# Expert token places cut from 256 to 240 in a fused linear-attention and mixture-of-experts kernel

## The chip, the cores and the metric

The kernel runs on one core of a Trainium2 chip. The metric is the device time of one execution in microseconds (us), and the time given for a kernel is the median of several runs. All profile times below are us from the start of the profiled span unless ns is written. PE is the matmul engine TensorE and PEld its weight load, DVE is VectorE, ACT is ScalarE, POOL is GpSimd, and SP is the engine that issues most transfers.

## The reference

A recurrence over 768 steps runs for 4 batches and 8 heads of width 48, and its output is read as 3072 tokens of 384 numbers. These tokens go through a mixture of 8 experts. A token is worked on only if its skip score is above zero. It then belongs to one expert, the one of the largest gate logit.

```
state = w_t * state + k_t v_t^T          # per batch and head, 768 steps
y_t   = r_t (state_before + (u * k_t) v_t^T)

do_compute = x @ w_skip > 0              # x: 3072 x 384
e_idx  = argmax(x @ w_gate)              # 8 experts
gate_w = softmax(x @ w_gate)[e_idx]
h      = max(x[mask_e] @ w1[e], 0)       # 384 -> 1024
y      = gate_w * (h @ w2[e])            # 1024 -> 384
out[do_compute] = x + y
```

Worked out from these lines and the inputs that the reference draws, 1514 of the 3072 tokens are worked on, and the eight experts get 194, 234, 156, 201, 198, 219, 156 and 156 of them.

## The kernel before

The first part of the kernel goes through 24 chunks of 128 tokens and computes the recurrence, the outputs and the gate logits. While it does so, a router gives every token that is worked on a place in its expert: place 0, 1, 2 and so on, in the order of the tokens. There are two tiles of 128 places for each expert, 256 in all (`CAP`). The list of tokens by place is `idr` for reading and `ids` for writing.

The second part is the experts, and the change touches only this part. `expert(e)` runs for e from 0 to 7. For each expert the tokens are gathered row by row from `out` by an indirect transfer (`gather`), one transfer for each tile `xg` of 128 places. `tokens(e)` turns the two tiles around on PE (`psX`, three transposes a tile) and splits the result into a high part `xTh` and a low part `xTl`, both of the type float32r (f32r). Weights are split in the same way by `split_slice`, 512 columns at a time, into `w1h`, `w1l`, `w2h` and `w2l`.

The first layer has 8 blocks `psH` of 128 hidden units. Each block is 9 matmuls (three 128-deep slices by the three products high*high, high*low, low*high), with a 128x128 block of weights as the stationary operand and 256 token columns as the moving one. ACT takes a finished block out of PSUM as `hh`, and DVE makes the low part `hl` from the same block. Four PSUM banks take turns for `psH`, so a block needs the bank that the block four before it left. The second layer is `psO`: for each of the two token tiles 24 matmuls with 128 token columns of `hh` or `hl` as the stationary operand and 384 columns of `w2` as the moving one. DVE then forms `fin` (gate times the sum, plus the token), and `scatter` on POOL writes the rows back to `out`.

Expert 0 is different. Its first 128 places are done ahead of time (`early_expert`), and its second tile uses plain float32 matmuls (`hidden`, line 133 in the profile).

The order of PE, ACT, DVE and POOL in this part is the order of the code. The weights of the expert after next are loaded by SP when the splits have left the raw tile.

Two tests at the end decide whether a slow general path runs instead. One of them asks whether any token's place is `CAP` or higher (`row_tests`). With the inputs drawn it is not taken.

Of the kernel before, what the change touches and what calls it, by code (L numbers as in the profile page):

```python
# [8 lines left out]
F32 = mybir.dt.float32  # L9
BF16 = mybir.dt.bfloat16  # L10
F32R = mybir.dt.float32r
# [10 lines left out]
P = 128  # L22
NT = B * S
# [4 lines left out]
NP = H // 2  # L28
KC = DM // P
FC = DF // P  # L30
CAP = 256
CW = P + 2
Q_MIN = 2.0 ** -60
TOL = 2e-5
# [1 line left out]
NHB = 11  # L36
# [20 lines left out]
def rwkv_moe_kernel(ctx, tc, wrk, wrk0, vN, uP, wgs, wgp, w12, cst, out):  # L57
    nc = tc.nc
# [28 lines left out]
    def split(dst_h, dst_l, src, eng=None):  # L87
        nc.scalar.copy(dst_h, src)  # L88
        (eng or nc.vector).tensor_tensor(dst_l, src, dst_h.bitcast(F32), op=ALU.subtract)  # L89

    def split_slice(e, i, eng=None):
        q, cs = i // 6, slice((i % 6) * 512, (i % 6 + 1) * 512)
        for k in (2 * q, 2 * q + 1):
            if (e, k) not in wsp:
                wtile(e, k)
        split(wsp[e, 2 * q][:, cs], wsp[e, 2 * q + 1][:, cs], raws[e, q][:, cs], eng)
# [20 lines left out]
    def drain(g):  # L117
        for _ in g:
            pass
# [3 lines left out]
    xg = {s: keep.tile([P, DM], F32, name=f"xg{s}") for s in range(4)}  # L123
# [7 lines left out]
    def hidden(ps, xT, fc, kc):  # L131
        o = kc * DF + fc * P
        return nc.tensor.matmul(ps, raws[0, 0][:, o:o + P], xT[:, kc], start=(kc == 0),  # L133
                                stop=(kc == KC - 1))
# [5 lines left out]
    with tc.tile_pool(name="att", bufs=2) as att, \  # L140
# [51 lines left out]
        ident = c_sb[:, C_ID:C_ID + P]  # L192
# [243 lines left out]

        idr = keep.tile([P, 2, E], U32, name="idr")

        def gather(s, pool):
            if pool:  # L440
                xg[s] = pool.tile([P, DM], F32, tag=f"xg{s}", name=f"xg{s}", bufs=1)
            return nc.gpsimd.indirect_dma_start(
                out=xg[s], out_offset=None, in_=out,
                in_offset=bass.IndirectOffsetOnAxis(ap=idr[:, s % 2, s // 2:s // 2 + 1], axis=0),
                bounds_check=NT - 1, oob_is_err=False)

        def router(i0, m):
# [319 lines left out]
        ids = keep.tile([P, 2, E], U32, name="ids")  # L767
        gates = keep.tile([P, 2, E], F32, name="gates")
        with tc.manual_schedule(engines={nc.tensor.engine, nc.scalar.engine, nc.vector.engine}):
# [9 lines left out]
            for k in range(done[0], 6 * FC - 4):  # L779
# [4 lines left out]
                                    axis=AX, op=ALU.add)  # L784
# [5 lines left out]
    with tc.tile_pool(name="wset1", bufs=1) as ws1, tc.tile_pool(name="moe", bufs=2) as moe, \  # L790
            tc.tile_pool(name="ps2", bufs=1, space=PSUM) as ps2:
        wset1[0] = ws1
        def pair(e, instr=None):
            for s in (2 * e, 2 * e + 1):
                ga = gather(s, moe)
                if instr is not None:
                    tc.add_manual_dep(ga.ins, instr.ins.name,
                                      mybir.DependencyInfo(mybir.DependencyClass.Sync,
                                                           mybir.DependencyReason.DATA),
                                      reason="pace")  # L800
# [8 lines left out]
        def tokens(e):  # L809
            xTh = moe.tile([P, KC, CAP], F32R, tag="xTh", name=f"xTh{e}")  # L810
            xTl = moe.tile([P, KC, CAP], F32R, tag="xTl", name=f"xTl{e}")
            for j in range(2):
                ps = ps1.tile([P, KC, P], F32, tag="psT", name=f"psX2{e}_{j}", bufs=2)
                for kc in range(KC):
                    nc.tensor.transpose(ps[:, kc], xg[2 * e + j][:, kc * P:(kc + 1) * P], ident)  # L815
                split(xTh[:, :, j * P:(j + 1) * P], xTl[:, :, j * P:(j + 1) * P], ps)
            xTs[e] = xTh, xTl

        def scatter(s, o):
            sc = nc.gpsimd.indirect_dma_start(  # L820
                out=out, out_offset=bass.IndirectOffsetOnAxis(ap=ids[:, s % 2, s // 2:s // 2 + 1],
                                                               axis=0),
                in_=o, in_offset=None, bounds_check=NT - 1, oob_is_err=False)
            tc.declare_no_dep(sc.ins, group="rows", reason="tokens are scattered to rows of their own")
            tc.add_to_no_dep_group("rows", sc.ins)

# [4 lines left out]
        def row_tests():  # L831
# [10 lines left out]
            nc.vector.tensor_reduce(vt[:, 2:3], rall[:, :, 0], axis=AX, op=ALU.max)  # L842
            nc.vector.tensor_scalar(vt[:, 2:3], vt[:, 2:3], float(CAP), None, op0=ALU.is_ge)
            nc.vector.scalar_tensor_tensor(vt[:, 3:4], vt[:, 1:2], B * NC - 0.5, vt[:, 2:3],
# [8 lines left out]
        def expert(e):  # L853
            todo = []
            if e + 1 < E:
                todo = list(range(0 if e > 0 else 6, 12))

            def more(k):
                for _ in range(k):
                    if todo:  # L860
                        split_slice(e + 1, todo.pop(0))


            h = {}
            nh = FC if e > 0 else FC // 2
            for q in range(nh):
                ps = (ps1 if q % 4 < 2 else ps2).tile(
                    [P, CAP], F32, tag=("psA0", "psA1", "psY", "psB")[q % 4], name=f"psH{e}_{q}")
                hh = moe.tile([P, CAP], F32R, tag="hh", name=f"hh{e}_{q}", bufs=NHB)
                hl = moe.tile([P, CAP], F32R, tag="hl", name=f"hl{e}_{q}", bufs=NHB)  # L870
                if e == 0:
                    for i in range(2):
                        ts = slice(i * P, (i + 1) * P)
                        for kc in range(KC):
                            hidden(ps[:, ts], xT0[1], 2 * q + i, kc)
                        h[1, 2 * q + i] = hh[:, ts], hl[:, ts]
                else:
                    w1h, w1l = wsp[e, 0], wsp[e, 1]
                    xTh, xTl = xTs[e]
                    for kc in range(KC):  # L880
                        o = kc * DF + q * P
                        nc.tensor.matmul(ps, w1h[:, o:o + P], xTh[:, kc], start=(kc == 0), stop=False)  # L882
                        nc.tensor.matmul(ps, w1h[:, o:o + P], xTl[:, kc], start=False, stop=False)  # L883
                        nc.tensor.matmul(ps, w1l[:, o:o + P], xTh[:, kc], start=False,  # L884
                                         stop=(kc == KC - 1))
                    for j in range(2):
                        ts = slice(j * P, (j + 1) * P)
                        h[j, q] = hh[:, ts], hl[:, ts]
                act = nc.scalar.activation(hh, ps, AF.Relu)  # L889
                if later_pairs and (e, q) != (0, 0):  # L890
                    pair(later_pairs.pop(0), act)
                    while first and not later_pairs:
                        scatter(*first.pop(0))
                nc.vector.scalar_tensor_tensor(hl, ps, 0.0, hh.bitcast(F32),  # L894
                                               op0=ALU.max, op1=ALU.subtract)
                more(1)
            if e + 1 < E:
                tokens(e + 1)
            if e == 0:
                first.append((0, fin0))  # L900
            w2h, w2l = wsp[e, 2], wsp[e, 3]
            for j in range(1 if e == 0 else 0, 2):
                pso = ps1.tile([P, DM], F32, tag=("psu", "pss")[j], name=f"psO{e}_{j}")
                for fc in range(FC):
                    o = slice(fc * DM, (fc + 1) * DM)
                    nc.tensor.matmul(pso, h[j, fc][0], w2h[:, o], start=(fc == 0), stop=False)  # L906
                    nc.tensor.matmul(pso, h[j, fc][0], w2l[:, o], start=False, stop=False)  # L907
                    nc.tensor.matmul(pso, h[j, fc][1], w2h[:, o], start=False,  # L908
                                     stop=(fc == FC - 1))
                more(2)  # L910
                if j == 0 and e in (1, 2):
                    (row_tests, verdict)[e - 1]()
                s = 2 * e + j
                o = moe.tile([P, DM], F32, tag="fin", name=f"fin{e}_{j}", bufs=3)
                nc.vector.scalar_tensor_tensor(o, pso, gates[:, j, e:e + 1], xg[s],  # L915
                                               op0=ALU.mult, op1=ALU.add)
                if later_pairs:
                    first.append((s, o))
                else:
                    scatter(s, o)  # L920
                if s == 2 * E - 3:
                    nc.gpsimd.drain()
                    verdicts.append(nc.values_load(flag_i[0:1, 0:1], min_val=0, max_val=2))
            more(12)
            if e + 2 < E:
                drain(load_weights(e + 2, 0))
                drain(load_weights(e + 2, 1))
# [170 lines left out]
```

## Time and profile before

| what | value |
|---|---|
| median of 3 runs | 286.65 us (286.0 to 287.15) |
| the profiled execution | 286.06 us |
| its span, first to last instruction | 284.2 us |
| PE busy | 271.2 us, 95% of the span |
| granted TensorE clock over the span | 0.999 of full speed |
| DVE, ACT, POOL busy | 217.0, 159.4, 145.9 us |
| memory traffic | 64.41 MB, mean 227 GB/s |

1.86 us of the profiled execution lie outside its span. The experts 1 to 7 take the stretch from 156.0 to 279.3 us. A matmul's record begins before the array is free for it, so the records of neighbours overlap; how long one matmul takes in a row of them is read from the distance of their starts, and not from the duration in the record. A plain float32 matmul leaves two records, each with a weight load of its own (48 such matmuls at line 133 stand as x96).

### The profile page before, as it was taken

The numbers are of one execution on the slowest core, as the hardware profiler recorded it, in microseconds if no ns is written. First come the engines' busy times: TensorE is split into PE (matmuls) and PEld (weight loads), VectorE is DVE, ScalarE is ACT, GpSimd is POOL, SyncE is SP. The second block draws the span as 40 slices with busy tenths as digits, with TensorE's granted clock in tenths as the row PEclk, the third lists the DMA queues.
The fourth block names the chain that finished last, engine by engine and source line by source line (L and its number), as shares of the span: only waits on it lengthen the run. The fifth ranks groups of instructions, "written<-read, shape, count | busy, mean of one in ns | idle before, by whom it ended". The sixth has DMA issues, their size and how long they took to land.

```text
span 284.2 us, 8967 instructions
## 1 busy us (share of the span) xinstructions
PE 271.2 (95%) x3601; PEld 248.9 (88%) x3602; DVE 217.0 (76%) x414; ACT 159.4 (56%) x464; POOL 145.9 (51%) x140
## 2 busy tenths in 40 slices
PE   6998999999999999999999999999999999999993
PEld 2687878788887888887999999999999999999992
DVE  7997999999989999972747697948859588595320
ACT  5175555787658957768416573827638276381310
POOL 4986775699978998974656625011030110201111
PEclk9999999999999999999999999999999999999999
DMA  7999999998999869992078997565672656700001
GB/s 217 239 311 333 277 345 339 363 332 246 297 278 302 252 218 348 308 310 65 28 256 294 345 314 267 212 213 200 221 258 68 231 200 221 268 5 28 10 5 41
DMA packets 26131, 64.41 MB, mean 227 GB/s; under 512 B 4342, under 2 KB 15386, under 8 KB 26080
## 3 DMA queue, kind: packets, MB, share of 16 engines
q1 hardware_dynamic: 23712, 58.14, 62.3%
q0 software_dynamic: 2048, 5.48, 5.9%
q8 instruction: 30, 0.49, 0.7%
q10 hardware_dynamic: 320, 0.13, 0.2%
q14 instruction: 21, 0.17, 0.2%
HBM read 56.69 MB, written 7.86 MB: 227 GB/s over the span
## 4 chain that ended last, share of the span: by engine, by line
PE 57%; POOL 8%; issue 6%; DVE 4%; ACT 3%; DMA 1%; POOLq 0%; DVEq 0%; ACTq 0%
PE psH L884 7%; PE psH L883 7%; PE psH L882 7%; PE psO L906 6%; PE psO L908 6%; PE psO L907 6%; PE psH L133 4%; PE psY L409 3%; POOL rp L336 2%; PE psA L358 2%; POOL kq L326 2%; PE psY L413 2%; PE psX L815 2%; PE psO L658 2%; PE psX L425 1%
## 5 line engine op out<-in xcount | busy, mean ns | idle before, releaser
L820 POOL DMA_INDIRECT out<-fin,ids x16 | 16.8, 1047 | 99.1 <-DVE fin L915 92.7
L889 ACT ACTIVATE hh<-psH 128x256 fp32r<-128x256 f32 x60 | 23.1, 385 | 56.6 <-PE psH L884 53.4
L884 PE MATMUL psH<-xTh,w1l 128*128 128x256 f32 x168 | 47.5, 283 | 0.0
L883 PE MATMUL psH<-xTl,w1h 128*128 128x256 f32 x168 | 47.5, 283 | 0.0
L882 PE MATMUL psH<-xTh,w1h 128*128 128x256 f32 x168 | 47.5, 283 | 0.0
L906 PE MATMUL psO<-w2h,hh 128*128 128x384 f32 x120 | 40.9, 341 | 0.0
L908 PE MATMUL psO<-w2h,hl 128*128 128x384 f32 x120 | 40.2, 335 | 0.0
L907 PE MATMUL psO<-w2l,hh 128*128 128x384 f32 x120 | 40.1, 335 | 0.0
L894 DVE SCALAR_TENSOR_TENSOR hl<-psH,hh 128x256 fp32r<-128x256 f32 x60 | 25.1, 418 | 13.3 <-ACT hh L889 12.0
L326 POOL TENSOR_TENSOR kq<-wrk,q 128x512 f32<-128x512 f32 x24 | 28.2, 1177 | 11.7 <-DVE q L309 3.5
L364 DVE TENSOR_TENSOR asb<-psA,c_sb 128x512 f32<-128x512 f32 x48 | 30.4, 676 | 3.5 <-PE psA L358 3.4
L331 DVE TENSOR_TENSOR_SCAN rh<-wrk,rowsk,pss 128x520 f32<-128x520 f32 x24 | 31.1, 1296 | 2.0
L318 POOL TENSOR_TENSOR rk<-wrk 128x512 f32<-128x512 f32 x24 | 31.0, 1292 | 2.4 <-DMA wrk<-wrk 2.4
L884 PEld LDWEIGHTS psH<-xTh,w1l 128*128 128x128 f32 x168 | 32.2, 192 | 0.0
L883 PEld LDWEIGHTS psH<-xTl,w1h 128*128 128x128 f32 x168 | 32.2, 192 | 0.0
L882 PEld LDWEIGHTS psH<-xTh,w1h 128*128 128x128 f32 x168 | 32.2, 191 | 0.0
L309 DVE TENSOR_TENSOR_SCAN q<-wrk,pss 128x520 f32<-128x520 f32 x24 | 29.5, 1230 | 3.0 <-DMA wrk<-wrk 0.9
L336 POOL TENSOR_TENSOR rp<-wrk,rh 128x512 f32<-128x512 f32 x23 | 27.2, 1181 | 5.4 <-DVE rh L331 5.0
L89 DVE TENSOR_TENSOR w2l<-r,w2h 128x512 fp32r<-128x512 f32 x42 | 27.7, 685 | 2.0 <-ACT w2h L88 1.4
L409 PE MATMUL psY<-asb,v 128*48 128x128 f32 x384 | 26.5, 276 | 2.6 <-DVE psY L381 2.3
L915 DVE SCALAR_TENSOR_TENSOR fin<-psO,gates,xg 128x384 f32<-128x384 f32 x15 | 9.3, 618 | 25.2 <-PE psO L908 24.6
L358 PE MATMUL psA<-rp,kq 64*64 64x128 f32 (+1 forms) x768 | 26.0, 251 | 1.8 <-issue 1.1
(154 smaller groups left out, 608.4 us busy)
## 6 DMA issues: line engine op xcount, KB each, us to landing
r<-w SPq DMA_DIRECT2D x48, 512.0 KB
wrk<-wrk SPq DMA_DIRECT2D x21, 772.5 KB
v<-vN SPq DMA_DIRECT2D x24, 192.0 KB
vt<-wrk SPq DMA_DIRECT2D x48, 96.0 KB
out<-x SPq DMA_DIRECT2D x24, 192.0 KB
wrk<-wrk SPq DMA_DIRECT2D x1, 579.4 KB
wrk<-wrk SPq DMA_DIRECT2D x1, 512.0 KB
wrk<-wrk SPq DMA_DIRECT2D x1, 384.0 KB
```

Source lines behind the costliest of these rows:

```text
L318: nc.gpsimd.tensor_tensor(work[i]["rk"].rearrange("p a j -> p (a j)"), t[:, R_OFF:K_OFF], t[:, K_OFF:V_OFF], op=ALU.mult)
L326: nc.gpsimd.tensor_tensor(kq, wk["k"], wk["q"][:, :, 1:1 + P], op=ALU.mult)
L331: nc.vector.tensor_tensor_scan(rh.rearrange("p a j -> p (a j)"), wk["w"][:, 0:NP * CW], reads_at[:, :NP * CW], rowsk, op0=ALU.mult, op1=AL ...
L336: eng.tensor_tensor(rp, wk["r"], rh[:, :, :P], op=ALU.mult)
L358: nc.tensor.matmul(psa[g][j:j + HP, a, j:], wk["kq"][rows, a, j:j + HP], wk["rp"][rows, a, j:], start=True, stop=True)
L409: nc.tensor.matmul(y_at(a, g), v[:, 2 * a + g], wk["asb"][g][:, a], start=False, stop=True, skip_group_check=True)
L882: nc.tensor.matmul(ps, w1h[:, o:o + P], xTh[:, kc], start=(kc == 0), stop=False)
L883: nc.tensor.matmul(ps, w1h[:, o:o + P], xTl[:, kc], start=False, stop=False)
L884: nc.tensor.matmul(ps, w1l[:, o:o + P], xTh[:, kc], start=False, stop=(kc == KC - 1))
L906: nc.tensor.matmul(pso, h[j, fc][0], w2h[:, o], start=(fc == 0), stop=False)
L907: nc.tensor.matmul(pso, h[j, fc][0], w2l[:, o], start=False, stop=False)
L908: nc.tensor.matmul(pso, h[j, fc][1], w2h[:, o], start=False, stop=(fc == FC - 1))
```

## The change

The constant `CAP` becomes 240. The first tile of an expert keeps 128 places and the second has 112. For the experts 1 to 7 everything that ran over 256 token columns runs over 240, and everything that ran over the second tile runs over 112 rows: the gather, the transposes, the two splits, the first layer's matmuls, `hh` and `hl`, the stationary operand of the second tile's `psO`, `fin` and the scatter. Expert 0 keeps 256 columns. The list of places still has 256 entries, of which the last 16 are not gathered. The test for the general path now asks for a place of 240 or higher.

```diff
-CAP = 256
+CAP = 240
...
+        def width(j):
+            return min(P, CAP - j * P)
+
         def gather(s, pool):
...
+            w = width(s % 2) if s > 1 else P
             return nc.gpsimd.indirect_dma_start(
-                out=xg[s], out_offset=None, in_=out,
-                in_offset=bass.IndirectOffsetOnAxis(ap=idr[:, s % 2, s // 2:s // 2 + 1], axis=0),
+                out=xg[s][:w], out_offset=None, in_=out,
+                in_offset=bass.IndirectOffsetOnAxis(ap=idr[:w, s % 2, s // 2:s // 2 + 1], axis=0),
...
-                    nc.tensor.transpose(ps[:, kc], xg[2 * e + j][:, kc * P:(kc + 1) * P], ident)
-                split(xTh[:, :, j * P:(j + 1) * P], xTl[:, :, j * P:(j + 1) * P], ps)
+                    nc.tensor.transpose(ps[:, kc, :w], xg[2 * e + j][:w, kc * P:(kc + 1) * P],
+                                        ident[:w, :w])
+                split(xTh[:, :, ts], xTl[:, :, ts], ps[:, :, :w])
...
         def scatter(s, o):
+            w = width(s % 2)
...
-                in_=o, in_offset=None, bounds_check=NT - 1, oob_is_err=False)
+                in_=o[:w], in_offset=None, bounds_check=NT - 1, oob_is_err=False)
...
+            n_ = CAP if e > 0 else 2 * P
...
-                    [P, CAP], F32, tag=("psA0", "psA1", "psY", "psB")[q % 4], name=f"psH{e}_{q}")
-                hh = moe.tile([P, CAP], F32R, tag="hh", name=f"hh{e}_{q}", bufs=NHB)
-                hl = moe.tile([P, CAP], F32R, tag="hl", name=f"hl{e}_{q}", bufs=NHB)
+                    [P, n_], F32, tag=("psA0", "psA1", "psY", "psB")[q % 4], name=f"psH{e}_{q}")
+                hh = moe.tile([P, 2 * P], F32R, tag="hh", name=f"hh{e}_{q}", bufs=NHB)[:, :n_]
+                hl = moe.tile([P, 2 * P], F32R, tag="hl", name=f"hl{e}_{q}", bufs=NHB)[:, :n_]
...
+                w = width(j) if e > 0 else P
+                po = pso[:w]
...
-                    nc.tensor.matmul(pso, h[j, fc][0], w2h[:, o], start=(fc == 0), stop=False)
+                    nc.tensor.matmul(po, h[j, fc][0], w2h[:, o], start=(fc == 0), stop=False)
...
-                nc.vector.scalar_tensor_tensor(o, pso, gates[:, j, e:e + 1], xg[s],
+                nc.vector.scalar_tensor_tensor(o[:w], po, gates[:w, j, e:e + 1], xg[s][:w],
```

The change moves no instruction on the way that the inputs take: on PE, DVE, ACT, POOL and SP every row stands where it stood, with the same names, and only sizes differ. On PE this is the end of expert 1's first layer, before (`psH` is the first layer, `psX` the transposes of expert 2's tokens, `psO` the second layer):

```order
L883 MATMUL psH_7_3059<-xTl_2869,w1h_1_2135 128x256
L884 MATMUL psH_7_3059<-xTh_2868,w1l_1_2136 128x256
L815 MATMUL psX_0_3077<-c_sb,xg_2777 128x128 x3
L815 MATMUL psX_1_3083<-c_sb,xg_2781 128x128 x3
L906 MATMUL psO_0_3089<-w2h_1_2801,hh_0_2922 128x384
```

And the same place now:

```order
L891 MATMUL psH_7_3059<-xTl_2869,w1h_1_2135 128x240
L892 MATMUL psH_7_3059<-xTh_2868,w1l_1_2136 128x240
L820 MATMUL psX_0_3077<-c_sb,xg_2777 128x128 x3
L820 MATMUL psX_1_3083<-c_sb,xg_2781 128x112 x3
L916 MATMUL psO_0_3089<-w2h_1_2801,hh_0_2922 128x384
```

Nothing moved; the first layer's matmuls have 240 columns and the second tile's transposes 112.

## Rows read from the trace of the kernel before

**Rows 1.** The page, part 1: busy us (share of the span) xinstructions of each engine.

```profile
PE 271.2 (95%) x3601; PEld 248.9 (88%) x3602; DVE 217.0 (76%) x414; ACT 159.4 (56%) x464; POOL 145.9 (51%) x140
```

**Rows 2.** Table by stretch: length, busy us (xinstructions) by engine, clock, DMA share, GB/s.

```profile
core 0: us, PE busy (x) PEld busy (x) DVE busy (x) ACT busy (x) POOL busy (x), PEclk, DMA share, GB/s
156.03:173.67 17.64, 17.64 (x128) 17.64 (x128) 13.93 (x34) 9.59 (x22) 9.23 (x9) 1.00 0.94 326
...
191.69:209.32 17.63, 17.63 (x127) 17.63 (x127) 12.87 (x24) 9.97 (x22) 2.16 (x2) 1.00 0.54 193
```

**Rows 3.** Groups of PE by shape: weights, output, count | busy us, mean ns | idle.

```profile
L884 PE MATMUL psH<-xTh,w1l 128*128 128x256 f32 x168 | 47.5, 283 | 0.0
L883 PE MATMUL psH<-xTl,w1h 128*128 128x256 f32 x168 | 47.5, 283 | 0.0
L882 PE MATMUL psH<-xTh,w1h 128*128 128x256 f32 x168 | 47.5, 283 | 0.0
...
L133 PE MATMUL psH<-xT,r 128*128 128x128 f32 x96 | 11.6, 277 | 0.0
```

**Rows 4.** Timeline of PE, expert 3's first layer: start us, us, what.

```profile
191.69 0.28 PE L882 MATMUL psH<-xTh,w1h 128*128 128x256 f32 x1
...
200.20 0.29 PE L884 MATMUL psH<-xTh,w1l 128*128 128x256 f32 x1
200.32 0.82 PE L815 MATMUL psX<-c_sb,xg 128*128 128x128 f32 x6
```

**Rows 5.** Timeline of PE, expert 7's second layer, first and last of 48.

```profile
270.84 0.34 PE L906 MATMUL psO<-w2h,hh 128*128 128x384 f32 x1
...
278.99 0.34 PE L908 MATMUL psO<-w2h,hl 128*128 128x384 f32 x1
```

**Rows 6.** Timeline of PEld, three runs of float32 weight loads.

```profile
82.37 0.97 PEld L425 LDWEIGHTS psX<-wgp_sb,xT 128*128 128x128 f32 x8
...
145.85 5.33 PEld L133 LDWEIGHTS psH<-xT,r 128*128 128x128 f32 x47
151.10 0.69 PEld L815 LDWEIGHTS psX<-c_sb,xg 128*128 128x128 f32 x6
```

**Rows 7.** Timeline of PE, the matmuls of the first of these.

```profile
82.39 1.12 PE L425 MATMUL psX<-wgp_sb,xT 128*128 128x105 f32 x8
```

**Rows 8.** Groups of PEld by shape, the first layer in f32r, then two float32 groups.

```profile
L882 PEld LDWEIGHTS psH<-xTh,w1h 128*128 128x128 f32 x168 | 32.2, 191 | 0.0
L425 PEld LDWEIGHTS psX<-wgp_sb,xT 128*128 128x128 f32 x192 | 23.4, 191 | 1.4 <-issue 1.0 <-ACT xT L418 0.5
...
L815 PEld LDWEIGHTS psX<-c_sb,xg 128*128 128x128 f32 x42 | 4.8, 140 | 0.0
```

**Rows 9.** Timeline of ACT, expert 1's first block, then expert 3's second.

```profile
159.17 0.38 ACT L889 ACTIVATE hh<-psH 128x256 fp32r<-128x256 f32 x1 [5.03 <-PE psH L884]
...
194.04 0.38 ACT L889 ACTIVATE hh<-psH 128x256 fp32r<-128x256 f32 x1 [0.19 <-PE psH L884]
```

**Rows 10.** Timeline of DVE, expert 1's first layer.

```profile
159.58 0.42 DVE L894 SCALAR_TENSOR_TENSOR hl<-psH,hh 128x256 fp32r<-128x256 f32 x1 [2.05 <-ACT hh L889]
...
160.70 0.42 DVE L894 SCALAR_TENSOR_TENSOR hl<-psH,hh 128x256 fp32r<-128x256 f32 x1
...
161.64 0.42 DVE L894 SCALAR_TENSOR_TENSOR hl<-psH,hh 128x256 fp32r<-128x256 f32 x1
```

**Rows 11.** Timeline of PE, expert 1: first matmul of the blocks 0, 4 and 5.

```profile
156.03 0.28 PE L882 MATMUL psH<-xTh,w1h 128*128 128x256 f32 x1
...
160.34 0.28 PE L882 MATMUL psH<-xTh,w1h 128*128 128x256 f32 x1
...
161.42 0.28 PE L882 MATMUL psH<-xTh,w1h 128*128 128x256 f32 x1
```

**Rows 12.** Timeline of the end, all engines.

```profile
279.37 0.62 DVE L915 SCALAR_TENSOR_TENSOR fin<-psO,gates,xg 128x384 f32<-128x384 f32 x1 [3.55 <-PE psO L908]
280.26 0.98 POOL L820 DMA_INDIRECT out<-fin,ids  x1 [3.18 <-DVE fin L915]
```

More of the change, by code (lines that the diff above doesn't have):

```diff
@@ L812, in tokens @@
             for j in range(2):
+                w, ts = width(j), slice(j * P, j * P + width(j))
                 ps = ps1.tile([P, KC, P], F32, tag="psT", name=f"psX2{e}_{j}", bufs=2)
                 for kc in range(KC):
-                    nc.tensor.transpose(ps[:, kc], xg[2 * e + j][:, kc * P:(kc + 1) * P], ident)
-                split(xTh[:, :, j * P:(j + 1) * P], xTl[:, :, j * P:(j + 1) * P], ps)
+                    nc.tensor.transpose(ps[:, kc, :w], xg[2 * e + j][:w, kc * P:(kc + 1) * P],
+                                        ident[:w, :w])
+                split(xTh[:, :, ts], xTl[:, :, ts], ps[:, :, :w])
             xTs[e] = xTh, xTl
         def scatter(s, o):
+            w = width(s % 2)
             sc = nc.gpsimd.indirect_dma_start(
-                out=out, out_offset=bass.IndirectOffsetOnAxis(ap=ids[:, s % 2, s // 2:s // 2 + 1],
+                out=out, out_offset=bass.IndirectOffsetOnAxis(ap=ids[:w, s % 2, s // 2:s // 2 + 1],
                                                                axis=0),
-                in_=o, in_offset=None, bounds_check=NT - 1, oob_is_err=False)
+                in_=o[:w], in_offset=None, bounds_check=NT - 1, oob_is_err=False)
             tc.declare_no_dep(sc.ins, group="rows", reason="tokens are scattered to rows of their own")
@@ L886, in expert @@
                     for j in range(2):
-                        ts = slice(j * P, (j + 1) * P)
+                        ts = slice(j * P, j * P + width(j))
                         h[j, q] = hh[:, ts], hl[:, ts]
@@ L903, in expert @@
                 pso = ps1.tile([P, DM], F32, tag=("psu", "pss")[j], name=f"psO{e}_{j}")
+                w = width(j) if e > 0 else P
+                po = pso[:w]
                 for fc in range(FC):
                     o = slice(fc * DM, (fc + 1) * DM)
-                    nc.tensor.matmul(pso, h[j, fc][0], w2h[:, o], start=(fc == 0), stop=False)
-                    nc.tensor.matmul(pso, h[j, fc][0], w2l[:, o], start=False, stop=False)
-                    nc.tensor.matmul(pso, h[j, fc][1], w2h[:, o], start=False,
+                    nc.tensor.matmul(po, h[j, fc][0], w2h[:, o], start=(fc == 0), stop=False)
+                    nc.tensor.matmul(po, h[j, fc][0], w2l[:, o], start=False, stop=False)
+                    nc.tensor.matmul(po, h[j, fc][1], w2h[:, o], start=False,
                                      stop=(fc == FC - 1))
```

## The prediction

> **What bounds the kernel now.** I read the page first, then a table by stretch, then the timeline of PE. PE is busy for 271.2 of 284.2 us [rows 1]. In the experts it never pauses: the stretch of expert 1 has 17.64 us of PE work in 17.64 us, that of expert 3 17.63 in 17.63 [rows 2], and the groups of the first layer show no idle time [rows 3]. DVE has 12.87 us of work in the same 17.63 us and ACT 9.97 [rows 2]; in the steady experts ACT sits for 0.19 us before each block until PE has finished it [rows 9]. So here a nanosecond taken out of PE's row of matmuls is a nanosecond off the end, until something else is late. The clock is 1.00 of full speed in these stretches [rows 2], that is the upper of its two levels, 2.4 GHz, and PE has no pause in them that could bring it down.
>
> The quantity that decides is not the 283 ns of a record but the distance from one matmul's start to the next. In expert 3 the first layer starts at 191.69 and the transposes behind it at 200.32; between lie 72 matmuls (8 blocks of 9), so one takes 8.63 / 72 = 119.9 ns [rows 4]. In expert 7's second layer the first and the last of 48 start 8.15 us apart, 8.15 / 47 = 173.4 ns each [rows 5]. Between 256 and 384 columns that is 53.5 ns for 128 columns, or 0.418 ns a column, one column a cycle at 2.4 GHz. What is left, 119.9 - 256 x 0.418 = 12.9 ns, is a fixed part that both widths have.
>
> **The first layer's matmuls** are the change's one large term. There are 3 x 168 = 504 of them [rows 3], and each loses 16 columns: 16 x 0.418 = 6.69 ns, from 119.9 to 113.2 ns. 504 x 6.69 ns = **3.37 us**, 0.48 us an expert for seven experts.
>
> No row shows an f32r matmul narrower than 256 columns, so 113.2 is a line drawn beyond its two points, and I bound it by what else a matmul needs, its weight load. Every matmul here loads 128x128 weights of its own. Where the matmuls are short, the loads set the distance: 8 loads in a row at line 425 take 0.97 us with the last one's own 0.191 in it, (0.97 - 0.191) / 7 = 111.3 ns, and the matmul behind them has 105 columns [rows 6 to 8]. At line 133 the columns are 128, 23 more, and the distance is (5.33 - 0.19) / 46 = 111.7 ns; in the transposes it is (0.69 - 0.14) / 5 = 110 ns, a load there being 140 ns [rows 6, 8]. So loads of this size follow each other every 110 to 112 ns, whatever runs over them. The load record of the first layer is 191 ns, the same as line 425's 191 [rows 8]. So the lower end for the distance is 110 ns, a gain of 504 x 9.9 ns = 5.0 us, and the upper end is 119.9, no gain, if f32r loads need what they need now. I take 113.2: it lies just above what the nearest rows give for the load alone, so the columns should still be what decides.
>
> The Trainium skill, "TensorE: Matmul & The Clock Gate", section "LDWEIGHTS (loading the stationary operand)", speaks against this change: a load's time goes by its columns divided by 1.2 GHz, 107 ns for 128 columns, however few token columns follow. By that, 240 columns (100 ns at the clock above) are shorter than the load under them, and narrowing below 256 buys nothing that the load does not allow. The rows of 110 to 112 ns agree with 107 ns and some nanoseconds for the handover; if the handover were the first layer's 12.9 ns, the load would allow 119.6 ns and the sum would be almost nothing. That case is the first rival below.
>
> **The rest of PE.** The second layer keeps 48 matmuls of 384 columns an expert; only the second tile's stationary operand shrinks from 128 to 112 columns. At 173.4 ns a matmul the load of about 111 ns lies inside it, so I count 0; a load that were shorter or longer by some ns would change nothing. The second tile's transposes get 112 columns. Their 110 ns is the load's, and the load still has 128 columns: 21 transposes, 0.
>
> **ACT and DVE.** `hh`, `hl`, the splits of the tokens and `fin` get a little shorter or stay the same, and lie beside PE's work. The cover is thinner than it was. A block will take 9 x 113.2 = 1.02 us where it took 1.08. DVE needs 0.94 us a block when it is catching up (159.58, 160.70, 161.64: 1.12 and then 0.94) [rows 10], so it still keeps up. One place is tight. In expert 1 ACT starts its first block at 159.17 [rows 9], some 1.9 us after that block's nine matmuls from 156.03 on, for a reason that the rows don't show and that the change need not shift. DVE leaves the banks of blocks 0 and 1 at 159.58 + 0.42 = 160.00 and 160.70 + 0.42 = 161.12 [rows 10]. PE wants them for the blocks 4 and 5, now at 160.34 and 161.42 [rows 11]; with the change at 156.03 + 36 x 0.1132 = 160.11 and 156.03 + 45 x 0.1132 = 161.12. So it just meets them: 0 to 0.1 us lost, once. I count 0.05.
>
> **Transfers.** Seven gathers and eight scatters issue no fewer instructions, each with 112 rows where it is a second tile's (expert 0's scatter too). Only the last scatter is on the path: `fin` 0.62 us, then POOL's 0.98 us, then the landing [rows 12]. 16 of 128 rows fewer would take at most 0.98 / 8 = 0.12 us off; a partition less costs DVE nothing. I count 0.05. The weights are the same bytes in a part that is 0.48 us an expert shorter. Expert 1's stretch has the transfers at 0.94 of their share and the steady experts at 0.54 [rows 2]; ACT and DVE reach their slices of the next weights earlier by no more than that half microsecond, and four banks of `psH` lie between them and PE. I count 0.
>
> **Sum.** 3.37 - 0.05 + 0.05 = 3.4 us. Against the profiled execution, 286.06 us, that is 282.7. The median of the runs shown lies 0.6 us above that execution, at 286.65, so I forecast **283.3** for the median.
>
> **Rivals.**
> *The load sets the distance, with the first layer's own handover.* At 256 columns and 2.4 GHz a matmul lasts as long as a load of the skill's length, so the rows at 256 and 384 can't tell which of the two the 12.9 ns follow. If they follow the load too, the distance stays near 119.9 and the time near 286.6. For it: f32r shows these 12.9 ns, and the plain float32 rows don't. Against it: three kinds of load at 110 to 112 ns. Between the two, at 116 ns, the gain is 504 x 3.9 = 2.0 us, 284.7. Chance of all this 0.17.
> *A matmul shorter than its load loses the overlap (slower).* If the next load no longer starts under the running matmul once the matmul is shorter than the load, each pays both: 111 + 113 = 224 ns in place of 119.9, 504 x 104 ns = 52 us, 339 us. It decides as soon as the columns take less time than the load, which 240 columns may do by a few ns. A plain float32 matmul is that dear: two records of 111.7 ns [rows 3, 6], 223 ns for 128 columns, and if the narrow f32r matmul ran in that way by columns, it would be dearer still (418 ns, 437 us). Against it: at line 425 the columns are the fewest, and the loads still follow each other without a gap. Chance 0.11.
> *The general path runs.* The change lowers the test from 256 to 240 places. The fullest expert has 234 tokens with the reference's inputs, so it stays off. If it ran, every tile of 128 tokens would read all weights again, 24 x 8 x 3 MB, over 2 ms at the page's 227 GB/s. Chance 0.01.
> *The gain is given back in stalls* (bank handovers, late weights). The tight place above costs 0.1 us; to lose 2 us it would take such a stall of 0.3 us in each of seven experts, where ACT now waits for PE. Chance 0.03, near 285.5.
>
> **How the numbers follow.** The forecast has 0.68, from 281.7 (the 110 ns end) to 284.3. The runs before spread by 1.1 us. The range goes from 281.7 to 287.2: it takes in both ends of the unknown distance, the first rival and the stalls, with half the spread above 286.6, and leaves out the slow cases (0.12). A measurement of this kernel can tell about 0.5%, 1.4 us, from no change. Faster by more than that is the forecast and the part of the first rival at 116 ns or less, 0.68 + 0.05 = 0.73. Within it are the rest of that rival and the stalls, 0.12 + 0.03 = 0.15. Slower is 0.12.
>
> **What would show it.** The first layer's starts should lie 113 ns apart, 72 of them in 8.15 us, with the second layer at 173 ns as before; an expert should take 17.15 us and the last PE record end 3.3 to 3.4 us earlier. At 119 to 120 ns the first rival is right; at 200 ns or more the second. A pause of PE before expert 1's block 4 or 5 would show the tight place, and idle time before `psH` in later experts the stalls. What stays most open is the one number that no row has, an f32r matmul below 256 columns.

## The result and the profile after

The changed kernel takes 283.09 us in the median of 5 runs (282.68 to 283.36), the kernel before 286.65 us (286.0 to 287.15, now 5 runs). The ratio of their times is 0.9874 with a 95% interval of 0.9855 to 0.9894, that is 3.6 us less. 283.3 us had been forecast.

The page of the changed kernel, part 1 (busy us, share of the span, xinstructions), answers to [rows 1]:

```profile
PE 267.2 (95%) x3601; PEld 244.8 (87%) x3602; DVE 215.7 (77%) x414; ACT 158.3 (56%) x464; POOL 147.1 (52%) x140
```

PE has 4.0 us less to do and the span is 3.3 us shorter (280.9 for 284.2). The table by stretch, for expert 1 and expert 3 as in [rows 2] with the same columns:

```profile
156.36:173.43 17.07, 17.07 (x128) 17.07 (x127) 13.67 (x34) 9.34 (x22) 7.42 (x7) 1.00 0.93 309
190.85:207.91 17.06, 17.06 (x128) 17.06 (x127) 12.68 (x24) 9.84 (x22) 2.14 (x2) 1.00 0.57 201
```

PE is as full as before, at the same clock, and an expert takes 17.06 us in place of 17.63. The timeline of PE in expert 3's first layer answers to [rows 4], and that of expert 7's second layer to [rows 5]:

```profile
190.85 0.27 PE L890 MATMUL psH<-xTh,w1h 128*128 128x240 f32 x1
...
198.81 0.28 PE L892 MATMUL psH<-xTh,w1l 128*128 128x240 f32 x1
198.93 0.49 PE L820 MATMUL psX<-c_sb,xg 128*128 128x128 f32 x3
...
267.22 0.34 PE L916 MATMUL psO<-w2h,hh 128*128 128x384 f32 x1
...
275.38 0.34 PE L918 MATMUL psO<-w2h,hl 128*112 128x384 f32 x1
```

72 matmuls in 198.93 - 190.85 = 8.08 us are 112.2 ns each, where it was 119.9. The seven first layers, read in this way, take 8.08 to 8.11 us (before: 8.63), together 56.70 in place of 60.40: **3.70 us**, 7.3 ns for each of the 504 matmuls. The second layer's matmul takes 8.16 / 47 = 173.6 ns, as before. The six groups of transposes take 0.55 us in place of 0.57, together 0.14 us. With 0.11 us in the second layers the experts are 3.95 us shorter from the first `psH` to the first `psO` of expert 7. Of that the profiled execution shows 3.3.

Two things take the rest. The part ahead of the experts, which the change doesn't touch, came 0.33 us later (the first `psH` at 156.36, before at 156.03). This differs from one execution to the next and doesn't go with the width: the experts begin between 155.4 and 158.7 in the other profiles shown here but for one (160.2). And from the last matmul's start to the end it took 5.52 us in place of 5.22. This is no accident of one execution: the two profiles whose last scatter has 128 rows (before, and bf16 with 256 columns, below) show 5.22 both times, the four with 112 rows 5.48 to 5.63.

So the experiments are best compared from the first `psH` to the end of the span, without the part ahead of it: 128.18 us before, 124.54 with the change, 3.64 us less.

### The profile page after: what moved, and what is told of

Same layout as the page of the kernel before. It is cut to its first block, busy times and chain, and to the rows that moved or that the text cites. A ratio compares the mean times of both kernels' runs of the same rounds, so it can differ in the third digit from the quotient of the medians.

```text
span 280.9 us, 8967 instructions
## 1 busy us (share of the span) xinstructions
PE 267.2 (95%) x3601; PEld 244.8 (87%) x3602; DVE 215.7 (77%) x414; ACT 158.3 (56%) x464; POOL 147.1 (52%) x140
## 4 chain that ended last, share of the span: by engine, by line
PE 51%; POOL 11%; issue 6%; DMA 4%; DVE 3%; ACT 3%; POOLq 0%; DVEq 0%; ACTq 0%; SPq 0%
PE psO L916 7%; PE psO L918 6%; PE psO L917 6%; PE psH L891 6%; PE psH L890 6%; PE psH L892 6%; PE psH L133 4%; POOL rp L336 3%; POOL kq L326 2%; DMA wrk<-wrk 2%; POOL rk L318 2%; POOL hot L534 2%; PE psO L662 2%; DMA v<-vN 2%; PE psX L820 2%
## 5 line engine op out<-in xcount | busy, mean ns | idle before, releaser
L897 ACT ACTIVATE hh<-psH 128x240 fp32r<-128x240 f32 (+1 forms) x60 | 22.4, 374 | 53.0 <-PE psH L892 46.8
L891 PE MATMUL psH<-xTl,w1h 128*128 128x240 f32 x168 | 46.3, 275 | 0.0
L890 PE MATMUL psH<-xTh,w1h 128*128 128x240 f32 x168 | 46.1, 275 | 0.0
L892 PE MATMUL psH<-xTh,w1l 128*128 128x240 f32 x168 | 46.1, 274 | 0.0
L916 PE MATMUL psO<-w2h,hh 128*128 128x384 f32 (+1 forms) x120 | 40.9, 341 | 0.0
L918 PE MATMUL psO<-w2h,hl 128*128 128x384 f32 (+1 forms) x120 | 40.3, 336 | 0.0
L917 PE MATMUL psO<-w2l,hh 128*128 128x384 f32 (+1 forms) x120 | 40.2, 335 | 0.0
L902 DVE SCALAR_TENSOR_TENSOR hl<-psH,hh 128x240 fp32r<-128x240 f32 (+1 forms) x60 | 24.2, 404 | 11.9 <-ACT hh L897 7.1
L925 DVE SCALAR_TENSOR_TENSOR fin<-psO,gates,xg 128x384 f32<-128x384 f32 (+1 forms) x15 | 9.3, 618 | 26.1 <-PE psO L918 23.9
```

Source lines behind the costliest of these rows:

```text
L916: nc.tensor.matmul(po, h[j, fc][0], w2h[:, o], start=(fc == 0), stop=False)
L917: nc.tensor.matmul(po, h[j, fc][0], w2l[:, o], start=False, stop=False)
L918: nc.tensor.matmul(po, h[j, fc][1], w2h[:, o], start=False, stop=(fc == FC - 1))
```

## Experiments

The experiments ask two things: which part of the change brings the gain, and whether the columns or the weight load set the distance of the first layer's matmuls. Below, the first layer of expert 3 is shown for each kernel: the start of its first matmul and of the transposes behind its 72nd.

**Undoing what stands ahead of the first layer.** The gather, the transposes and the splits go back to whole tiles.

```diff
-            w = width(s % 2) if s > 1 else P
+            w = P
...
-            xTh = moe.tile([P, KC, CAP], F32R, ...)
+            xTh = moe.tile([P, KC, 2 * P], F32R, ...)
...
-                w, ts = width(j), slice(j * P, j * P + width(j))
+                w, ts = P, slice(j * P, j * P + P)
...
-                        nc.tensor.matmul(ps, w1h[:, o:o + P], xTh[:, kc], ...)
+                        nc.tensor.matmul(ps, w1h[:, o:o + P], xTh[:, kc, :n_], ...)
```

> The gathers, the transposes and the splits of the tokens go back to 128 rows and 256 columns; the first layer keeps its 240 columns and the second tile its 112 rows from the second layer on. My theory: the gain is the first layer's columns alone, so the first layer's starts stay 112.5 ns apart, and the time is 283.1 to 283.4, with 0 to 0.2 us lost in the six groups of transposes. The rival, that what precedes the first layer (shorter gathers and splits) brings a part of the gain, wants 284 or more.

Measured: 0.9921 of the kernel before (0.9882 to 0.9959), 284.42 us beside 287.05 on that chip. Timeline of PE:

```profile
191.01 0.27 PE L890 MATMUL psH<-xTh,w1h 128*128 128x240 f32 x1
...
199.08 0.49 PE L820 MATMUL psX<-c_sb,xg 128*128 128x128 f32 x3
```

8.07 us, 112.1 ns: the first layer keeps its whole gain, and the transposes are back at 0.57 us a group. The time alone doesn't decide. 284.42 us lies past the 284 named for the rival, but this kernel's six executions go from 282.4 to 284.9, and the kernel before took 287.05 in place of 286.65 here. The interval holds the 0.9912 that the changed kernel has on a second chip (below) and just misses its 0.9874. The profile decides: from the first `psH` to the end it takes 124.48 us, as the changed kernel does (124.54). So what stands ahead of the first layer brings nothing beyond the 0.14 us of the transposes.

**The second layer alone.** Beside the edit above, the first layer goes back to 256 columns.

```diff
-            n_ = CAP if e > 0 else 2 * P
+            n_ = 2 * P
```

> Only the second layer's second tile is narrowed (112 token columns as stationary operand, 112 rows of fin and of the scatter); the first layer is back at 256 columns. My theory: no change, 286.3 to 286.9, the second layer's starts 173.4 ns apart with 112 columns of weights as with 128, the first layer's 119.9. The rival, that a shorter weight load or a shorter last scatter is worth something, wants 286.0 or less; if a load of 112 columns were dearer than one of 128, 287 or more.

Measured: 1.0004 (0.9972 to 1.0036), 287.23 us beside 287.05.

```profile
192.09 0.28 PE L890 MATMUL psH<-xTh,w1h 128*128 128x256 f32 x1
...
200.71 0.49 PE L820 MATMUL psX<-c_sb,xg 128*128 128x128 f32 x3
```

8.62 us again, and no change of the time: 112 rows in the second tile's `psO`, `fin` and scatter bring no gain. From the first `psH` to the end it takes 128.49 us, 0.3 more than the kernel before, most of it behind the last matmul (5.48 us for 5.22). The gain is the first layer's.

**Fewer columns still.** The constant changes, the test for the general path is held at 256, and expert 0's scatter goes back to 128 rows. Three widths were run, and tokens whose place is cut off are left as they came.

```diff
-CAP = 240
+CAP = 224
...
-            nc.vector.tensor_scalar(vt[:, 2:3], vt[:, 2:3], float(CAP), None, op0=ALU.is_ge)
+            nc.vector.tensor_scalar(vt[:, 2:3], vt[:, 2:3], 256.0, None, op0=ALU.is_ge)
...
-            w = width(s % 2)
+            w = width(s % 2) if s > 1 else P
```

> 224 places instead of 240, with the test for the general path held at 256, so that tokens with a place of 224 or higher are left as they came (part of the work is left out). My theory: the columns decide only down to the load, and loads follow each other every 110 to 112 ns, so the first layer's starts come 110 to 112 ns apart and the time is 281.8 to 282.9. If the columns alone decide, 105.5 ns apart, 504 x 7 ns = 3.5 us less than with 240, 279.6. If the load carries the first layer's own handover of 12.9 ns, it would have shown at 240 already. If a matmul shorter than its load loses the overlap, 200 ns or more apart and 325 us or more.

> 192 places, otherwise as with 224 (more tokens are left out). My theory: no gain behind 224, the starts 110 to 112 ns apart, about 282.3. Columns alone: 92 ns apart, 273. Overlap lost: 200 ns or more apart, 325 us or more.

> 160 places, otherwise as with 224 and 192 (still more tokens are left out). My theory: the load sets the distance, 111 to 112 ns, 8.0 us for a first layer. The rival, that the next load no longer starts under the running matmul once the matmul is much shorter than the load: two thirds of the columns of 240 would be the place to show it, with 200 ns or more, 14 us or more for a first layer.

Measured, in this order (timelines of PE of the three kernels; the first took 0.9892 of the kernel before, 0.9837 to 0.9947):

```profile
191.10 0.26 PE L890 MATMUL psH<-xTh,w1h 128*128 128x224 f32 x1
...
199.13 0.49 PE L820 MATMUL psX<-c_sb,xg 128*128 128x128 f32 x3
```

```profile
192.63 0.25 PE L890 MATMUL psH<-xTh,w1h 128*128 128x192 f32 x1
...
200.65 0.49 PE L820 MATMUL psX<-c_sb,xg 128*128 128x128 f32 x3
```

```profile
190.36 0.23 PE L890 MATMUL psH<-xTh,w1h 128*128 128x160 f32 x1
...
198.37 0.49 PE L820 MATMUL psX<-c_sb,xg 128*128 128x128 f32 x3
```

8.03, 8.02 and 8.01 us, or by the trace's nanoseconds 111.6, 111.4 and 111.2 ns a matmul. From 240 down to 160 columns, a third less, a matmul gets about 1 ns shorter. So there is a floor, and the changed kernel stands on it but for a nanosecond. The times say little: 283.26 us with 224 columns, where 281.8 to 282.9 had been expected, and 284.79 and 282.22 us in the single executions of the other two. The slow rival is out: even with 160 columns (67 ns at 0.418 ns a column) the next load runs under the matmul before it.

**Is the floor the load?** The same 192 columns, but the operands are read as bf16, the upper two bytes of each float32r number.

```diff
+        def top(z):
+            return z.bitcast(BF16)[:, 1::2]
...
-                        nc.tensor.matmul(ps, w1h[:, o:o + P], xTh[:, kc], ...)
+                        nc.tensor.matmul(ps, top(w1h)[:, o:o + P], top(xTh[:, kc]), ...)
```

> As with 192 places, but the first layer reads the upper two bytes of its float32r operands, weights and tokens, as bf16, so that its values are cut to bf16 (that part of the computation is changed, and tokens with a place of 192 or higher are left out). The columns are the same 192, the weight load is another. My theory, that the float32r load sets the 111.4 ns found with 192 columns: the bf16 load's record is shorter (98 ns or less in place of 190), so the columns decide again, near 12.9 + 192 x 0.418 = 93 ns a matmul, and the first layer takes 6.7 us in place of 8.02. The rival, that some fixed cost of PE and not the load sets the 111 ns: 111 ns here too, 8.0 us.

Measured, the timeline of PE, and below it the group of PEld by shape (count | busy us, mean ns):

```profile
190.16 0.26 PE L893 MATMUL psH<-xTh,w1h 128*128 128x192 bf16 x1
...
196.30 0.49 PE L820 MATMUL psX<-c_sb,xg 128*128 128x128 f32 x3
```

```profile
L893 PEld LDWEIGHTS <-w1h 128*128 128x128 bf16 x168 | 16.1, 96 | 1.4 <-issue 1.4
```

6.14 us, 85.2 ns a matmul. The load's record is 96 ns where the float32r one had 191 [rows 8], and the floor of 111 ns is gone with it. The fixed part is 85.2 - 80.3 = 4.9 ns, not the 12.9 of the forecast's line. The single execution took 272.79 us beside 287.94 for the kernel before; in expert 1 PE waited twice for DVE (0.44 and 0.17 us), which no float32r kernel here shows.

This edit changes the tokens' type with the weights', so by itself it doesn't tell which of the two made the floor. A row of the kernel before does, for plain float32. At line 390 two streams of matmuls alternate, both with 48 token columns, one with 64 columns of weights and one with 48. In the trace the first stream's starts come 58 to 59 ns apart, the second's 45, from the second matmul of each on. Apart from the columns of weights, and where the result goes, nothing differs. The loads' records go the same way (groups of PEld by shape in the kernel before; the first line is a load of a single column):

```profile
L850 PEld LDWEIGHTS psf<-vt,c_sb 128*1 128x1 f32 x2 | 0.1, 81 | 0.0
...
L390 PEld LDWEIGHTS psu<-v,kt 128*64 128x64 f32 x160 | 10.8, 137 | 2.3 <-ACT kt L350 0.4
L390 PEld LDWEIGHTS psu<-v,kt 128*48 128x48 f32 x160 | 8.7, 124 | 0.0
```

Less the 81 ns of the single column, the records of 124, 137 and 191 ns are 43, 56 and 110 ns, and the distances are 45, 58 and 111. So the load's length goes with the distance in all of these rows, the first layer's among them. No run changes the float32r weights without the tokens, so for float32r the load is the cause that the rows bear out, not one that was isolated.

**The curve between 240 and 256.** Three widths more, edited as above.

> 248 places, otherwise as with 224 (no token has a place that high, so nothing is left out). If the columns decide down to 240, a straight line from 119.8 ns at 256 to 112.5 at 240 puts this at 116.1, 8.36 us for a first layer. If 240 is already held by the load and the line with 0.418 ns a column runs down to it, 116.5 ns, 8.39 us. If there is a step just below 256, it is at 112 ns here already, 8.1 us.

> 232 places, otherwise as with 224 (two tokens are left out). My theory: the load's 111.4 to 111.6 ns, 8.03 us for a first layer. If the columns still decided below 240, 109 ns, 7.85 us.

> 252 places, otherwise as with 248 (nothing is left out). Between 256 (119.8 ns) and 248 (113.3 to 114.9 ns) the distance fell by 4.9 to 6.5 ns, where 8 columns at 0.418 ns are 3.3. If columns at 0.418 ns are what counts here, 118.1 ns, 8.51 us for a first layer. If an extra of 2 to 3 ns falls away as soon as the matmul is shorter than its load, 115 to 116 ns, 8.3 us. If it falls away evenly, 116.5 to 117.4 ns, 8.4 us.

Measured with 248, 232 and 252 columns, timelines of PE:

```profile
190.66 0.27 PE L890 MATMUL psH<-xTh,w1h 128*128 128x248 f32 x1
...
198.92 0.49 PE L820 MATMUL psX<-c_sb,xg 128*128 128x128 f32 x3
```

```profile
190.34 0.27 PE L890 MATMUL psH<-xTh,w1h 128*128 128x232 f32 x1
...
198.39 0.38 PE L820 MATMUL psX<-c_sb,xg 128*128 128x128 f32 x2
```

```profile
195.37 0.28 PE L890 MATMUL psH<-xTh,w1h 128*128 128x252 f32 x1
...
203.78 0.38 PE L820 MATMUL psX<-c_sb,xg 128*128 128x128 f32 x2
```

8.26, 8.05 and 8.41 us (8.419 in the trace), or 114.7, 111.8 and 116.9 ns. The seven first layers of a kernel are not all alike; the second row of the table has the lowest and the highest of them.

| columns | 256 | 252 | 248 | 240 | 236 | 232 | 224 | 192 | 160 |
|---|---|---|---|---|---|---|---|---|---|
| ns a matmul, expert 3 | 119.9 | 116.9 | 114.7 | 112.2 | 111.8 | 111.8 | 111.6 | 111.4 | 111.2 |
| lowest and highest of seven | 119.8, 119.9 | 116.1, 116.9 | 113.3, 114.9 | 112.2, 112.6 | 111.8, 112.1 | 111.6, 111.8 | 111.5, 111.6 | 111.4, 111.4 | 111.1, 111.2 |
| 0.418 ns a column + 12.9 | 119.9 | 118.2 | 116.6 | 113.2 | 111.5 | 109.9 | 106.5 | 93.2 | 79.8 |

The measured distance falls faster than the line at first, then lies flat. None of the three expectations for 248 columns came out (116.1, 116.5 and 112 ns). With 252 columns four first layers lie at 116.9, in the range named for an even decline, and three at 116.1, just above the 115 to 116 named for a step; the line's 118.1 is out. Why the first layers of one kernel differ by up to 1.6 ns isn't shown.

**The fixed part with a shorter load.** The bf16 reading with all 256 columns.

> The first layer with all 256 columns, its float32r operands read as bf16 by their upper two bytes (its values are cut to bf16). With 192 columns this took 85.2 ns, that is 80.3 for the columns and 4.9 of a fixed part. If the 12.9 ns of the float32r matmul come with its load, the fixed part is 4.9 ns here too: 106.9 + 4.9 = 111.9 ns, 8.05 us for a first layer. If 12.9 ns come with the width, 119.8 ns, 8.63 us.

Measured, timeline of PE:

```profile
193.43 0.29 PE L893 MATMUL psH<-xTh,w1h 128*128 128x256 bf16 x1
...
201.61 0.49 PE L820 MATMUL psX<-c_sb,xg 128*128 128x128 f32 x3
```

8.18 us, 113.6 ns, 6.6 above the 107.0 of its columns; 111.9 had been expected from the load, 119.8 from the width. So about half of the 12.9 ns goes away with the bf16 reading at the same width. Whether the weights' type or the tokens' takes it away, and what makes up the rest, isn't settled.

**A place or two fewer, and the change once more.**

```diff
-CAP = 240
+CAP = 236
```

> 236 places, which the fullest expert of 234 still fits, with the test for the general path at 236. My theory: the load holds the distance at 111.5 to 112 ns in place of 112.5, so the gain over 240 is 504 x 0.5 to 1.0 = 0.2 to 0.5 us, too little to tell. If the columns still decided, 504 x 1.7 = 0.8 us.

> The changed kernel once more, on the same chip as the one with 236 places: 0.987 of the kernel before, as found, and 112.5 ns between the first layer's starts.

Measured on one chip beside a kernel before of 286.87 us: 236 places 0.9884 (0.9849 to 0.9919), 240 places 0.9912 (0.9883 to 0.9941). Timelines of PE:

```profile
191.27 0.27 PE L890 MATMUL psH<-xTh,w1h 128*128 128x236 f32 x1
...
199.32 0.49 PE L820 MATMUL psX<-c_sb,xg 128*128 128x128 f32 x3
```

```profile
189.88 0.27 PE L890 MATMUL psH<-xTh,w1h 128*128 128x240 f32 x1
...
197.96 0.49 PE L820 MATMUL psX<-c_sb,xg 128*128 128x128 f32 x3
```

8.05 and 8.08 us. The intervals overlap, and the 0.3 us that seven first layers give are too little to tell, so 236 isn't shown to be better. The changed kernel's 0.9912 is a smaller gain than the 0.987 expected of it, though the intervals of its two measurements overlap. Its profile agrees with the first: 124.66 us from the first `psH` to the end (124.54). What 240 left is nearly nothing.

## Why the prediction was right, and where it was not

The forecast of 283.3 us was right, with 283.09 measured. The sum behind it, 3.4 us, is near the 3.64 us found from the first `psH` to the end, but its parts are not: the first layers gave 3.70 for 3.37, the transposes and the second layers 0.14 and 0.11 for nothing, and the end took 0.3 us where 0.05 was to be won.

*PE bounds the experts, and what it saves comes off the end.* Right: the stretches have no pause in either kernel, and undoing the parts shows that the first layer carries the gain (8.07 us and 0.9921 with everything ahead of it undone, 1.0004 without it).

*504 x 6.69 ns = 3.37 us.* Nearly right in size, 3.70 us measured (7.3 ns), and not for the reason given. The step that failed is "the columns should still be what decides". At 240 columns they hardly do: the line gives 113.2 ns, the kernel takes 112.2 to 112.6, and with 232 to 160 columns it takes 111.8 to 111.1. From 256 to 248 columns the distance falls by 5.2 ns in expert 3 where the line has 3.3, and from 240 to 160 by 1 ns where the line has 33. The two errors, a distance that falls faster than the line just below 256 and a floor that stops it just below 240, nearly cancel at this width. That is luck. Had the change gone to 224 places, the line would have promised 504 x 13.4 = 6.8 us, and the floor from the loads at lines 425 and 133 would have been the better guide: 111.3 and 111.7 ns there [rows 6], 111.1 to 111.8 here.

*The load as the bound of the gain.* The first rival was half right: the load does set the distance. The Trainium skill has a rule for it ("TensorE: Matmul & The Clock Gate", section "LDWEIGHTS (loading the stationary operand)"): a load's time is its columns of weights divided by 1.2 GHz, which is 107 ns for 128 columns. For the float32r weights the trace agrees with it, 111.2 ns with 160 token columns, some 4 ns more; for the bf16 reading it does not, 85.2 ns with 128 columns of weights too. The rival's condition was wrong: the 12.9 ns of the wide matmuls don't come on top of the load.

*The lost overlap.* Wrong down to 160 columns, as shown above.

*The transposes count 0.* They gave 0.14 us, gone when they were undone. "Their 110 ns is the load's" was wrong. In expert 3's group the last distance between two transposes of the second tile is 109 ns with 128 rows, 102 with 120, 95 with 112, 89 with 104 and 82 with 96, about 0.84 ns for each row fewer, while the load has 128 columns in all of them. Whether a row counts here in the weights or in what runs over them can't be told, since both have it. So the transposes were no third witness for the load's 110 to 112 ns; their load records are 140 ns and not 191 [rows 8]. The loads at lines 425 and 133 were.

*The second layer, `fin` and the scatter count 0 or nearly.* Right for PE: 173.6 ns with 112 columns of weights, and no gain from them alone.

*The tight place in expert 1.* It cost nothing. The rows of ACT, DVE and PE that answer to [rows 9 to 11]:

```profile
159.17 0.37 ACT L897 ACTIVATE hh<-psH 128x240 fp32r<-128x240 f32 x1 [4.78 <-PE psH L892]
```

```profile
159.58 0.41 DVE L902 SCALAR_TENSOR_TENSOR hl<-psH,hh 128x240 fp32r<-128x240 f32 x1 [1.31 <-ACT hh L897]
...
160.69 0.40 DVE L902 SCALAR_TENSOR_TENSOR hl<-psH,hh 128x240 fp32r<-128x240 f32 x1
```

```profile
160.41 0.27 PE L890 MATMUL psH<-xTh,w1h 128*128 128x240 f32 x1
...
161.42 0.27 PE L890 MATMUL psH<-xTh,w1h 128*128 128x240 f32 x1
```

DVE left the two banks at 159.99 and 161.09, PE began their next blocks at 160.41 and 161.42, in its even step. The experts began 0.33 us later in this execution, while DVE left the banks at the same times as before; without that the margin would have been near nothing, as counted. Two more profiles with 240 columns, that with the front undone and the repeat, show no pause there either (8.07 and 8.11 us for this first layer).

*The end.* Wrong in sign. The timeline of POOL, the last scatter, which answers to [rows 12]:

```profile
276.65 0.95 POOL L827 DMA_INDIRECT out<-fin,ids  x1 [3.17 <-DVE fin L925]
```

`fin` takes 0.62 us as before and POOL 0.95 for 0.98, but from there to the end of the span (280.89 us) it is 3.29 us, before 284.21 - 281.24 = 2.97. The prediction counted 0.05 us off for 16 rows fewer. POOL gave 0.03, and what follows it grew by 0.28 to 0.44 us in all four profiles with 112 rows. It isn't a matter of rows alone: from the last matmul's start to the end the kernels with 32 and 64 rows take 5.2 to 5.3 us, that with 108 rows 5.76. The runs don't show why.

## What to carry to other kernels

Before narrowing a row of matmuls, read two distances from the trace: that of the matmuls to be narrowed, and that of the shortest matmuls whose weights have the same shape and whose load records are as long. The second is the floor to expect. Here it left 8 ns of 120 to win and no more, whatever the width. A line through two wide shapes tells the slope between them, not what happens where the matmul becomes as short as its load; there one look at a width beyond the planned one says more than the line. And when two executions begin their changed part at different times, compare them from there on.

## What the runs showed of the hardware that was not expected

*The fixed part of a matmul is not the same for all types.* It is 12.9 ns at 256 and 384 columns of float32r, 4.9 and 6.6 ns at 192 and 256 columns of bf16.

*A gather of 124 rows was slow.* The kernel with 252 places took 291.43 us in its one execution, 4.6 above the kernel before on that chip. Its second tiles have 124 rows. The wait list of PE, and the page's row of the queue that gathers and scatters:

```profile
PE psX L820 <- DMA xg<-out,idr: 2.2, 1, 2.2
```

```profile
q0 software_dynamic: 3840, 5.45, 7.1%
```

PE sat 2.2 us for expert 1's second tile, which no other kernel here shows, and the queue has 3840 packets where the kernels with 128, 120, 112, 108 and 104 rows all have 2048. Its last scatter was slow too: 7.83 us from the last matmul's start to the end, in every other profile 5.2 to 5.8. The Trainium skill, "DMA: Bandwidth & Descriptors", section "Why a DMA increments its semaphore by 16 and not by 1", has a rule that fits this: a transfer is spread over the largest number of engines, up to 16, that divides its outermost sizes. By it that is 4 for 124 rows, and 15, 16, 12 and 13 for 120, 112, 108 and 104. No run here counts the engines, and the rule doesn't give the 0.3 us that the last scatter loses with 112 rows, since it has 16 engines for them as for 128. The rest of this execution's extra time, ahead of the experts, isn't explained.

*Transposes of very few rows took longer.* With 64 and 32 rows in the second tile a group of six transposes took 0.75 and 0.73 us, with 112 rows 0.55 and with 96 rows 0.52.
